# Infini-attention and feed-forward block: score maxima from 32-row products of the high parts, softmax sums from the numerators

## The chip, the cores and the metric

The kernel runs on one core of a Trainium2 chip. The metric is the device time of one execution in microseconds (us); lower is better. A core has five engines that matter here, each working through its own instructions in order: TensorE (PE in the profile, with its weight loads shown apart as PEld), VectorE (DVE), ScalarE (ACT), GpSimd (POOL), and SyncE (SP), which in this kernel issues the DMA transfers.

## The reference

A transformer block on 2048 tokens of width 1024. A modulation vector scales and shifts a layer norm; then attention with 32 heads of width 32, in four segments of 512 tokens, each with a compressed memory of the segments before; an output product; a second norm; a gated feed-forward of width 3584. What the change touches is the softmax of one segment:

```
for s in range(N):
    qs, ks, vs = q[:, :, s], k[:, :, s], v[:, :, s]
    logits = jnp.einsum("bhqd,bhkd->bhqk", qs, ks) * scale + mask
    p = _softmax(logits, axis=-1)
    a_dot = jnp.einsum("bhqk,bhkd->bhqd", p, vs)
    ...
    a_mem = num / den
    o = g * a_mem + (1.0 - g) * a_dot
```

## The kernel before, in words

All activations stand transposed, with the feature in the partitions. Products that need precision are made of high and low parts: a float32 number is cut into a rounded part (hi, type fp32r) and the rest (lo), and hi*hi, hi*lo and lo*hi are summed. An fp32r product streams its columns once; plain float32 products (the ones with `pt`, `mz`, `pk`) stand in the profile as two instructions for each product.

Attention is done in 32 steps: four heads (a group, 128 features) by one segment of 512 tokens. Round n of the loop in `attention` interleaves three things: the projections of step n+1 (`K0` to `K7` keys and values, `Q0` to `Q3` queries), the scores and maxima of step n (`scores`), and the probabilities and outputs of step n-1 (`values`), with the memory's products, the cuts of later weights, and in some rounds norms and loads of other stages. The order in a round is written out by hand, token by token, in `ORDER`; one string of tokens sets the order in each engine's queue at once, SP's and POOL's too.

The tokens that matter, with their lines:

- `kt` (`turned`, L412 to L421): the keys are transposed on PE; ACT writes the high part `kh`, DVE the low part `kl`. `qo` (`parts`, L442 to L451) does the same for the queries.
- `dk`, `dq` (`spread`, L403 to L406): three DMA transfers each put high, high and low parts into rows 0, 3, 6, ... and 1, 4, ... and 2, 5, ... of the first 96 partitions of `ks` and `qs`, so that one product over 96 rows sums the three partial products for one head. The weights' columns are arranged (`by_head`) so that the four heads of a group lie in the free dimension there.
- `S0` to `S3` (`rows`, L530 to L545): for 128 queries and each of four heads, one product over 96 rows with 256, 256, 384 or 512 keys (L540), then DVE adds the mask and takes the row's maximum (L542, output in `sj`, and the accumulator's result in `mm`), then ACT takes the exponential with that maximum and sums it into `ll` (L544). Each of the four writes a PSUM bank of its own, out of five that all small products share (`s_ps`).
- `tm`, `tq` (`maxima` L547, `to_queries` L557): the maxima, cut in two parts, are turned and put by DVE into rows 96 to 127 of `qs` (L559), which meet selecting rows in `ks`.
- `tr` (`shares` L563): one over the sums, times one minus the gate, spread on ACT (L568).
- `T0` to `T3` (L626 to L636): the scores again, transposed, keys in the partitions, over all 128 rows, so that the maximum is subtracted by the product itself; ACT takes the exponential into `pt` (L633), POOL clears the half above the diagonal (L634).
- `P0`, `P2` (`PV`, L638 to L644): values times `pt`, four heads side by side in four groups of 32 array columns (L643), 64 such groups of products in all.
- `rt` (`factors`, L652): PE turns the shares (L649) and ACT copies them; `rm` (L656) multiplies the output by them; `yt` adds the memory's part; `zs` stores.

`PV` is the only place in which products with fewer than 128 output rows lie side by side; `S` is the only one with fewer than 128 contraction rows (96).

## Time and profile before

| | us |
|---|---|
| median of 3 runs | 2741.93 (2741.18 to 2743.84) |
| profiled execution | 2742.03 |
| its span in the profile | 2740.3 |
| 28 of the 32 attention steps, 101.4 to 894.0 | 792.6 |
| PE busy in these | 792.03 |
| DVE busy in these | 555.40 |
| ACT busy in these | 579.28 |

The span is the time from the first to the last profiled instruction. Busy time is the union of an engine's instructions; since PE's instructions overlap in its pipeline, a busy PE may still wait inside, and what an instruction costs there is read from the distance between starts. The attention steps run from about 65 us to 980 us; what follows is the output product, the second norm and the feed-forward, which the change doesn't touch.

### The profile page before, as it was taken

The numbers are of one execution on the slowest core, as the hardware profiler recorded it, in microseconds if no ns is written. First come the engines' busy times: TensorE is split into PE (matmuls) and PEld (weight loads), VectorE is DVE, ScalarE is ACT, GpSimd is POOL, SyncE is SP. The second block draws the span as 40 slices with busy tenths as digits, with TensorE's granted clock in tenths as the row PEclk, the third lists the DMA queues.
The fourth block names the chain that finished last, engine by engine and source line by source line (L and its number), as shares of the span: only waits on it lengthen the run. The fifth ranks groups of instructions, "written<-read, shape, count | busy, mean of one in ns | idle before, by whom it ended". The sixth has DMA issues, their size and how long they took to land.

```text
span 2740.3 us, 43048 instructions
## 1 busy us (share of the span) xinstructions
PE 2715.1 (99%) x14748; PEld 2284.0 (83%) x14748; DVE 1556.0 (57%) x3516; ACT 1202.7 (44%) x2811; POOL 852.5 (31%) x1446
## 2 busy tenths in 40 slices
PE   7999999999999999999999999999999999999999
PEld 6888888888888888888888888888888888888887
DVE  7677667666776745555555555334433254575456
ACT  6777777676767634333333233111111033233323
POOL 4333334433333534254455452443541000000000
PEclk9999999999999999999999999999999999999999
DMA  7454445435443568778898678999998687795563
GB/s 261 131 148 135 129 126 150 125 108 151 113 131 101 158 210 295 251 290 326 310 351 310 263 281 276 361 362 353 363 358 313 219 316 252 264 307 197 185 207 123
DMA packets 244890, 637.77 MB, mean 233 GB/s; under 512 B 24768, under 2 KB 49344, under 8 KB 244672
## 3 DMA queue, kind: packets, MB, share of 16 engines
q1 hardware_dynamic: 244672, 635.03, 68.1%
q8 instruction: 116, 1.90, 0.3%
q14 instruction: 102, 0.84, 0.1%
HBM read 372.79 MB, written 211.81 MB: 213 GB/s over the span
## 4 chain that ended last, share of the span: by engine, by line
PE 96%; DMA 2%; DVE 1%; issue 0%; POOL 0%; ACT 0%; SPq 0%; DVEq 0%; POOLq 0%; ACTq 0%
PE f L1139 37%; PE y L1353 19%; PE kv L383 12%; PE y L714 6%; PE q L389 6%; PE S L540 3%; PE T L631 3%; PE O L643 3%; PE num L599 1%; PE M L582 1%; PE kv L512 1%; DMA ru<-wu 1%; PE tpb L266 1%; PE kT L417 0%; PE R L649 0%
## 5 line engine op out<-in xcount | busy, mean ns | idle before, releaser
L1139 PE MATMUL f<-A,B 128*128 128x512 f32 x4704 | 1072.7, 390 | 0.4 <-DVE c L1164 0.4
L1139 PEld LDWEIGHTS f<-A,B 128*128 128x128 f32 x4704 | 881.4, 188 | 184.8 <-DVE c L1164 1.1
L1353 PE MATMUL y<-B,L 128*128 128x512 f32 x2352 | 533.3, 389 | 0.0
L1353 PEld LDWEIGHTS y<-B,L 128*128 128x128 f32 x2352 | 441.4, 188 | 91.7
L544 ACT ACTIVATE sj<-sj,mm 128x384 f32<-128x384 f32 (+3 forms) x512 | 281.4, 552 | 49.4 <-DVE mm L542 49.1
L542 DVE CUSTOM_DVE_ANT_0 sj<-S,mask 128x384 f32<-128x384 f32 (+3 forms) x512 | 228.0, 488 | 106.2 <-PE S L540 81.3
L634 POOL TENSOR_SCALAR_AFFINE_SELECT pt<-pt 128x128 f32<-128x128 f32 x512 | 164.1, 345 | 293.9 <-ACT pt L633 287.6
L853 ACT ACTIVATE L<-X 128x512 fp32r<-128x512 f32 x168 | 105.8, 630 | 257.2 <-PE y L1353 167.0
L633 ACT ACTIVATE pt<-T 128x256 f32<-128x256 f32 (+3 forms) x512 | 181.9, 443 | 69.3 <-PE T L631 63.5
L383 PE MATMUL kv<-w,hhh 128*128 128x256 f32 x1024 | 199.6, 285 | 0.0
L855 DVE TENSOR_TENSOR L<-X,L 128x512 fp32r<-128x512 f32 x168 | 115.9, 691 | 145.8 <-ACT L L853 145.6
L1173 ACT ACTIVATE g<-g 128x512 f32<-128x512 f32 x56 | 35.4, 631 | 369.4 <-DVE g L1172 369.4
L374 POOL TENSOR_TENSOR w<-r,w 128x256 fp32r<-128x256 f32 x180 | 134.2, 781 | 158.6 <-ACT w L368 156.9
L383 PE MATMUL kv<-w,hha 128*128 128x256 f32 x896 | 177.4, 286 | 1.9 <-DVE vx L401 1.9
L1078 POOL TENSOR_TENSOR rw<-rw,gbb 128x256 f32<-128x256 f32 x112 | 91.4, 853 | 248.6 <-DMA rw<-wd 184.8
L383 PEld LDWEIGHTS kv<-w,hhh 128*128 128x128 f32 x1024 | 164.8, 191 | 1.4 <-issue 0.4
L383 PEld LDWEIGHTS kv<-w,hha 128*128 128x128 f32 x896 | 145.8, 192 | 4.1 <-DVE vx L401 2.2
L383 PE MATMUL kv<-w,hlh 128*128 128x256 f32 x512 | 144.7, 283 | 0.0
L383 PE MATMUL kv<-w,hla 128*128 128x256 f32 x448 | 127.0, 283 | 0.0
L714 PE MATMUL y<-wo,hho 128*128 128x512 f32 x384 | 125.9, 394 | 0.0
L1160 ACT ACTIVATE g<-f 128x512 f32<-128x512 f32 x56 | 33.5, 598 | 206.0 <-PE f L1139 206.0
L540 PE MATMUL S<-ks,qs 96*128 96x256 f32 (+2 forms) x512 | 110.4, 333 | 0.3
(244 smaller groups left out, 4150.1 us busy)
## 6 DMA issues: line engine op xcount, KB each, us to landing
bc_d<-B SPq DMA_DIRECT2D x189, 512.0 KB, 5.4
...
X<-hid_d SPq DMA_DIRECT2D x112, 256.0 KB, 4.8
wr<-gd_d SPq DMA_DIRECT2D x84, 256.0 KB, 4.1
qs<-qh SPq DMA_DIRECT2D x64, 256.0 KB, 3.6
```

Of the source, the lines that this page charges most:

```text
L374: nc.gpsimd.tensor_sub(w[:, 1, c], r[:, c], f32(w[:, 0, c]))
L383: nc.tensor.matmul(ps, b[:, sl], w[:, a], start=(kt == 0 and a == 0 and b is hi), stop=(kt == KT - 1 and a == 1), **kw)
L389: nc.tensor.matmul(ps, w[:, a], b, start=(kt == 0 and a == 0 and b is hi), stop=(kt == KT - 1 and a == 1), **kw)
L540: nc.tensor.matmul(ps[:, :nk], qs[:96, j, i * P:(i + 1) * P], ks[:96, j, :nk], start=True, stop=True)
L542: nc.vector.tensor_tensor_reduce(out=sj[:, :nv], in0=ps[:, :nv], in1=mask[:, L - nv:], scale=-1.0, scalar=3.4e38, op0=ALU.add, op1=ALU.min ...
L544: nc.scalar.activation(sj[:, :nv], sj[:, :nv], AF.Exp, bias=mm[:, j, i:i + 1], scale=-1.0, accum_out=ll[:, i, j:j + 1])
L633: nc.scalar.activation(pt, ps[:, nn - n:nn], AF.Exp)
L634: nc.gpsimd.affine_select(pt[:, :P], pt[:, :P], pattern=[[1, P]], compare_op=ALU.is_ge, fill=0.0, base=0, channel_multiplier=-1)
L714: nc.tensor.matmul(ps, b[:, i * P:(i + 1) * P], w[:, a, g % 2], start=(g == 0 and a == 0 and b is hi), stop=(g == G - 1 and a == 1))
L855: eng.tensor_sub(lo[:, k], src[:, k], f32(hi)[:, k])
L1139: nc.tensor.matmul(ps, B[m, i][:, a, kt * P:(kt + 1) * P], A[p, i, kt][b], start=(start and kt == 0 and a == 0 and b == 0), stop=(kt == 3 ...
L1353: nc.tensor.matmul(banks[t], ops[k][:, y, t * P:(t + 1) * P], B[slots[k]][:, x], start=(i not in (2, 4, 3) and j == 0 and x == 0 and y == ...
```

## The change

- `S` multiplies the high parts alone, straight from `kh` and `qh` (32 rows for each head, at partitions 0, 32, 64 and 96), with no copies by DMA. The columns of the weights are arranged so that a head's 32 features lie together. DVE adds the mask and takes the maximum as before, but writes its main output back to PSUM; `sj`, ACT's exponentials of it, and `ll` are gone. The maximum need not be exact, since numerators and sum now use the same one.
- The sums come from the numerators: `p1` to `p3` add `pt` of the later key blocks to that of the first (DVE), and `rt` multiplies them by a matrix of ones (four heads in four groups of 32 array columns). DVE turns the result, takes the reciprocal and turns it back; `rm` multiplies by it and by one minus the gate (`omc`). `tr`, the turns and the copies of the shares are gone.
- `dk`, `dq` now write the parts to DRAM (`aside`); the transfers into `ks` and `qs` (`fk`, `fq`) follow a round later and read from DRAM, 256 KB each.
- `tq` moves from DVE to ACT.
- `pt` has four tags of exact sizes; high and low parts have tags of their own.
- All orders are written anew.

The diff, with the old orders left out:

```diff
@@ -152,6 +152,7 @@
     omg = pa.tile([P, H], F32, name="omg")
+    omc = pa.tile([P, G], F32, name="omc")
     ones = cs([P, P], "ones")
@@ -348,7 +349,7 @@
-    hT, W, Mst, ST, SC, SY, PK = {}, {}, {}, {}, {}, {}, {}
+    hT, W, Mst, ST, HI, SY, PK, LATE = {}, {}, {}, {}, {}, {}, {}, {}
     ks_t = []
@@ -400,10 +401,14 @@
-    def spread(dst, parts):
-
-        for row, part in parts:
-            nc.sync.dma_start(f32(dst[row:96:3]), f32(part))
+    def aside(tiles, nm):
+        for c in "hl":
+            t = tiles[c + "d"] = dram.tile([P, L], F32, name=f"{c}{nm}_d", tag=nm[0] + c, bufs=2)
+            nc.sync.dma_start(t, f32(tiles[c]))
+
+    def spread(dst, tiles, rows):
+        for row, c in rows:
+            nc.sync.dma_start(f32(dst[row:96:3]), tiles[c + "d"].rearrange("(j d) t -> d j t", j=4))
@@ -415,8 +420,9 @@
                 nc.tensor.transpose(ps[:, t * P:(t + 1) * P], kn[:, t], ident)
-            kh = tiles["h"] = t2("kh" + nm, "sp", bufs=4, dt=F32R)
-            kl = tiles["l"] = t2("kl" + nm, "sp", bufs=4, dt=F32R)
+            kh = tiles["h"] = t2("kh" + nm, "hi", bufs=3, dt=F32R)
+            kl = tiles["l"] = t2("kl" + nm, "lo", bufs=2, dt=F32R)
+            HI.setdefault(n, {})["k"] = kh
             nc.scalar.activation(kh, ps, AF.Copy)
@@ -432,7 +438,8 @@
         u["kt"] = turned
-        u["dk"] = lambda: spread(ks, ((0, tiles["h"]), (1, tiles["h"]), (2, tiles["l"])))
+        u["dk"] = lambda: aside(tiles, "k" + nm)
+        LATE[n, "k"] = lambda: spread(ks, tiles, ((0, "h"), (1, "h"), (2, "l")))
         u["ek"] = expo
@@ -441,14 +448,14 @@
             ps = get()
-            qh = tiles["h"] = t2("qh" + nm, "sp", bufs=4, dt=F32R)
-            ql = tiles["l"] = t2("ql" + nm, "sp" if n else "sj", bufs=4 if n else 3, dt=F32R)
+            qh = tiles["h"] = t2("qh" + nm, "hi", bufs=3, dt=F32R)
+            ql = tiles["l"] = t2("ql" + nm, "lo", bufs=2, dt=F32R)
+            HI.setdefault(n, {})["q"] = qh
             nc.scalar.activation(qh, ps, AF.Copy, scale=SCALE)
...
             nc.vector.scalar_tensor_tensor(ql, ps, SCALE, f32(qh), op0=ALU.mult, op1=ALU.subtract)
-            ST[n][0] = t2("qs" + nm, "qs", bufs=2, dt=F32R, shape=(P, 4, L))
@@ -460,7 +467,12 @@
         u["qo"] = parts
-        u["dq"] = lambda: spread(ST[n][0], ((0, tiles["h"]), (2, tiles["h"]), (1, tiles["l"])))
+        u["dq"] = lambda: aside(tiles, "q" + nm)
+        def late():
+            ST[n][0] = t2("qs" + nm, "qs", bufs=2, dt=F32R, shape=(P, 4, L))
+            spread(ST[n][0], tiles, ((0, "h"), (2, "h"), (1, "l")))
+
+        LATE[n, "q"] = late
         u["ea"] = expo
@@ -528,21 +540,19 @@
         def rows(i):
-            qs, ks = ST[n][:2]
+            qh, kh = HI[n]["q"], HI[n]["k"]
             if i == 0:
                 d["mm"] = t2("mm" + nm, "mm", bufs=2, shape=(P, 4, 4))
-                d["ll"] = t2("ll" + nm, "ll", bufs=2, shape=(P, 4, 4))
-            mm, ll = d["mm"], d["ll"]
+            mm = d["mm"]
             nk = max(256, (i + 1) * P)
             nv = (i + 1) * P
+            ps = [s_ps(f"S{nm}_{j}{i}") for j in range(4)]
             for j in range(4):
-                ps = s_ps(f"S{nm}_{j}{i}")
-                nc.tensor.matmul(ps[:, :nk], qs[:96, j, i * P:(i + 1) * P], ks[:96, j, :nk], start=True, stop=True)
-                sj = t2(f"sj{nm}_{j}{i}", "sj", bufs=3)
-                nc.vector.tensor_tensor_reduce(out=sj[:, :nv], in0=ps[:, :nv], in1=mask[:, L - nv:], scale=-1.0,
+                h = slice(DH * j, DH * (j + 1))
+                nc.tensor.matmul(ps[j][:, :nk], qh[h, i * P:(i + 1) * P], kh[h, :nk], start=True, stop=True)
+            for j in range(4):
+                nc.vector.tensor_tensor_reduce(out=ps[j][:, :nv], in0=ps[j][:, :nv], in1=mask[:, L - nv:], scale=-1.0,
                                                scalar=3.4e38, op0=ALU.add, op1=ALU.min, accum_out=mm[:, j, i:i + 1])
-                nc.scalar.activation(sj[:, :nv], sj[:, :nv], AF.Exp, bias=mm[:, j, i:i + 1], scale=-1.0,
-                                     accum_out=ll[:, i, j:j + 1])
@@ -556,23 +566,14 @@
             for i in range(4):
-                nc.vector.tensor_scalar(ST[n][0][96:128, :, i * P:(i + 1) * P],
-                                        d["tt"][96:128].unsqueeze(1).to_broadcast([32, 4, P]),
-                                        seli[96:128, i:i + 1], None, op0=ALU.mult)
-
-        def shares():
-            rc = t2("rc" + nm, "rc", bufs=2, shape=(P, 4, 4))
-            nc.vector.reciprocal(rc, d["ll"])
-            nc.vector.tensor_mul(rc, rc, omg[:, 4 * g:4 * g + 4].unsqueeze(1).to_broadcast([P, 4, 4]))
-            rx = t2("rx" + nm, "rx", shape=(P, 4, 4, DH))
-            nc.scalar.activation(rx, rc.unsqueeze(3).to_broadcast([P, 4, 4, DH]), AF.Copy)
-            SC[n] = [rx, None]
+                nc.scalar.activation(ST[n][0][96:128, :, i * P:(i + 1) * P],
+                                     d["tt"][96:128].unsqueeze(1).to_broadcast([32, 4, P]),
+                                     AF.Identity, scale=seli[96:128, i:i + 1])
...
         u["tq"] = to_queries
-        u["tr"] = shares
@@ -629,7 +630,7 @@
                 nc.tensor.matmul(ps[:, :nn], ks[:, j, kc * P:(kc + 1) * P], qs[:, j, L - nn:], start=True, stop=True)
-                pt = t2(f"pt{nm}_{j}{kc}", f"pt{kc % 2}", bufs=4, shape=(P, L - kc % 2 * P))[:, :n]
+                pt = t2(f"pt{nm}_{j}{kc}", f"pt{kc}", bufs=4, shape=(P, n))
                 nc.scalar.activation(pt, ps[:, nn - n:nn], AF.Exp)
@@ -649,12 +650,24 @@
+        def added(kc):
+            for j in range(4):
+                t = pts[0, j][:, kc * P:]
+                nc.vector.tensor_add(t, t, pts[kc, j])
+
         def factors():
+            ps = s_ps("l" + nm)
+            for j in range(4):
+                nc.tensor.matmul(ps[32 * j:32 * j + 32], ones[:, :DH], pts[0, j], start=True, stop=True,
+                                 skip_group_check=True)
             d["r"] = tmp_tile("R" + nm)
-            nc.scalar.activation(d["r"], turned(SC[n][0], "R"), AF.Copy)
+            nc.vector.transpose(d["r"], ps)
+            rc = t2("rc" + nm, "rc", bufs=2, shape=(P, 16))
+            nc.vector.reciprocal(rc, d["r"].rearrange("p (b r) -> p b r", r=32)[:, :, 0])
+            nc.vector.transpose(d["r"], rc.unsqueeze(2).to_broadcast([P, 16, 32]))
...
         def scaled():
-            nc.vector.tensor_mul(d["r"], d["o"], d["r"])
+            nc.vector.scalar_tensor_tensor(d["r"], d["o"], omc[:, g:g + 1], d["r"], op0=ALU.mult, op1=ALU.mult)
@@ -663,6 +676,8 @@
         u["P2"] = lambda: PV(2)
+        for kc in (1, 2, 3):
+            u[f"p{kc}"] = lambda kc=kc: added(kc)
         u["rt"] = factors
@@ -1414,54 +1429,54 @@
...
+            "fk fq N K K N G1 K N N G2 K G0 K S0 S1 C1 S2 K S3 C2 K l1 l2 A tm tq L1 K K L2 K",
         (1,):
...
+            "fk K0 T0 ns K1 T1 K2 K3 K4 S0 P0 D0 o0 nc T2 p1 mz K5 p2 T3 K6 p3 n0 n1 m0 A rt Q0 nd S1 P2 K7 S2 m1 Q1 Q2 "
+            "rm S3 o1 fq yt zs Q3 kt qo tm nu ek ea ne dn dk nl tq dq eb",
         (2, 4, 6, 8):
...
+            "K0 K1 K2 Q0 S0 K3 G2 S1 fk ns wd o0 Q1 G1 T0 Q2 T1 Q3 nc C2 S2 P0 T2 K4 p1 T3 p2 qo fq G0 K5 C1 S3 ea p3 l2 "
+            "tm K6 P2 n0 eb n1 nd L2 nl l1 A K7 rt o1 rm kt dk ne L1 ek tq yt zs wl dq",
         (3, 5, 7):
...
+            "K0 K1 K2 S0 K3 T0 ns D0 K4 S1 K5 m0 T1 o0 A P0 p1 m1 mz T2 K6 T3 Q0 fk p2 nc S2 K7 p3 Q1 S3 P2 rt o1 Q2 nu "
+            "Q3 wl wd fq qo n0 tm ea n1 rm nl kt dn nd ek dk ne tq eb yt zs dq",
         (9,):
...
+            "K0 K1 K2 D0 S0 mz K3 T0 o0 K4 S1 K5 m0 T1 Q0 m1 S2 fk fq P0 T2 p1 Q1 S3 K6 Q2 p2 Q3 tm T3 K7 P2 p3 o1 kt rt "
+            "qo ea dk eb rm nu A dn ek dq yt zs tq",
         (10, 12):
...
+            "K0 G2 G1 K1 K2 S0 K3 A T0 C1 K4 wd S1 K5 o0 T1 Q0 S2 P0 T2 Q1 T3 K6 fk C2 p1 p2 p3 fq l2 S3 K7 P2 o1 kt dk "
+            "L2 l1 G0 rt L1 Q2 Q3 wl rm tm qo ea ek yt eb wl tq dq zs",
         (11, 13):
...
+            "D0 K0 S0 m0 wd K1 K2 T0 K3 S1 mz Q0 o0 fk Q1 S2 m1 wd K4 T1 Q2 S3 P0 wl p1 Q3 T2 K5 T3 p2 qo p3 fq tm ea K6 "
+            "eb K7 rt P2 o1 dq kt rm A ek tq yt dk nu zs dn",
         (14,):
...
+            "x wd wd K0 x K1 G2 x T0 K2 T1 x P0 x fk p1 T2 C2 x K3 G1 o0 l2 p2 S0 x K4 K5 T3 p3 S1 x P2 K6 x K7 S2 rt x "
+            "Q0 Q1 x o1 C1 x L2 kt fq dk S3 l1 x Q2 x G0 Q3 rm tm A qo ek dq L1 yt zs ea tq eb",
         (15,):
...
+            "K0 K1 S0 x D0 K2 fk A K3 S1 K4 S2 K5 fq m0 x x o0 T0 Q0 x T1 x Q1 mz m1 S3 P0 tm p1 Q2 T2 Q3 T3 p2 wd p3 K6 "
+            "qo x ea P2 K7 nu o1 dn dq eb kt rt tq rm yt dk x zs ek",
         (16,):
...
+            "x G1 x K0 Q0 T0 mz wl Q1 x T1 x Q2 S0 P0 x fk T2 p1 C1 G2 K1 S1 Q3 p2 K2 fq T3 l1 K3 wd p3 P2 qo o0 ea L1 S2 "
+            "K4 K5 S3 wl K6 G0 rt eb C2 tm K7 A rm nu o1 kt tq dk yt wl dq zs l2 L2 ek dn",
         (17,):
...
+            "fk K0 K1 K2 D0 m0 S0 T0 wd K3 S1 Q0 T1 Q1 m1 mz o0 S2 P0 p1 T2 p2 K4 T3 K5 p3 S3 K6 fq rt Q2 tm Q3 qo ea K7 "
+            "eb P2 o1 rm kt yt ek dq dk nu dn zs tq",
         (18, 20, 22, 24, 26, 28):
...
+            "K0 K1 K2 S0 K3 S1 wd K4 G1 T0 C1 G2 mz K5 S2 o0 K6 T1 P0 T2 Q0 fk T3 p1 K7 C2 p2 p3 S3 P2 o1 rt rm kt l1 fq "
+            "yt Q1 ek dk l2 Q2 tm nu dn Q3 G0 qo ea tq L2 zs wl L1 eb A dq",
         (19, 21, 23, 25, 27):
...
+            "wl D0 K0 K1 S0 K2 wd mz T0 wd K3 T1 K4 S1 P0 T2 p1 p2 K5 m0 T3 p3 K6 S2 P2 fk K7 wl o0 rt S3 o1 m1 Q0 Q1 rm "
+            "kt Q2 tm yt Q3 qo ea ek fq nu dn dk zs dq eb tq",
         (29,):
...
+            "K0 K1 S0 D0 wd K2 m0 m1 T0 K3 T1 K4 mz S1 P0 T2 K5 T3 p1 p2 K6 p3 o0 S2 Q0 P2 S3 Q1 rt K7 Q2 o1 tm rm fk kt "
+            "Q3 yt nu fq qo ea dk dn zs ek tq eb dq",
         (30,):
...
+            "x x K0 wo fk K1 S0 K2 ga mz wd T0 x x wo x K3 x o0 T1 fq K4 S1 P0 T2 p1 ga T3 p2 Q0 p3 x ga S2 P2 Q1 wp rt "
+            "wl K5 wp S3 x K6 K7 Q2 o1 wo Q3 x tm rm qo kt yt ea ek nu wl x dn x dk zs eb A dq tq x x wl wo",
         (31,):
...
+            "K0 K T0 T1 wp K1 S0 fk Q0 P0 wp T2 p1 S1 mz K2 p2 T3 S2 p3 K3 fq P2 K4 K5 S3 rt K6 rm yt tm Q1 nu tq dn zs "
+            "Q2 K7 K Q3",
         (32,):
...
+            "K0 K1 T0 K2 Q0 Q1 T1 K3 P0 T2 p1 p2 K4 T3 K5 p3 Q2 P2 rt rm yt K6 zs K7 Q3",
     }
@@ -1479,7 +1494,7 @@
             for h in range(2):
-                tag, bufs = ("pt0", 4) if h == 0 else ("sj", 3) if i < 3 else ("pq", 2)
+                tag, bufs = ("pt0", 4) if h == 0 else ("hi", 3) if i < 3 else ("pq", 2)
                 t = t2(f"x0_{i}_{h}", tag, bufs=bufs)
@@ -1515,6 +1530,9 @@
         nc.vector.tensor_scalar(omg, gall, -1.0, 1.0, op0=ALU.mult, op1=ALU.add)
+        own = omg.rearrange("p (g j) -> p g j", j=4)
+        nc.vector.tensor_mul(own, own, sel4.unsqueeze(1).to_broadcast([P, G, 4]))
+        nc.vector.tensor_reduce(omc, own, axis=AX.X, op=ALU.add)
         row = row_parts(scb, scol, tmp_tile, "sc")
@@ -1607,6 +1625,8 @@
             if n < len(steps):
+                for c in "kq":
+                    u["f" + c] = LATE.pop((n, c), None) or (lambda n=n, c=c: LATE.pop((n, c))())
                 scores(u, n, *steps[n][1:])
@@ -1648,7 +1668,7 @@
         pick = tmp_tile("pick")[:, :P].rearrange("p (j d) -> p j d", d=DH)
-        nc.gpsimd.affine_select(pick, ones.rearrange("p (j d) -> p j d", d=DH), pattern=[[-1, 4], [-4, DH]],
+        nc.gpsimd.affine_select(pick, ones.rearrange("p (j d) -> p j d", d=DH), pattern=[[-DH, 4], [-1, DH]],
                                 compare_op=ALU.is_equal, fill=0.0, base=0, channel_multiplier=1)
@@ -1692,7 +1712,7 @@
     def by_head(w):
-        return np.asarray(w).reshape(D, G, 4, DH).transpose(0, 1, 3, 2)
+        return np.asarray(w).reshape(D, G, 4, DH)
```

32 lines of the change are left out of this document (removed).

## The prediction

> **What bounds the kernel now.** I read the page first: its busy shares and the chain that ended last.
>
> ```profile
> span 2740.3 us, 43048 instructions
> PE 2715.1 (99%) x14748; PEld 2284.0 (83%) x14748; DVE 1556.0 (57%) x3516; ACT 1202.7 (44%) x2811; POOL 852.5 (31%) x1446
> PE 96%; DMA 2%; DVE 1%; issue 0%; POOL 0%; ACT 0%; SPq 0%; DVEq 0%; POOLq 0%; ACTq 0%
> ```
>
> PE is busy nearly all the span and holds 96% of the chain. Then the stretches: the 28 attention steps from 101.4 to 894.0 us, by busy time (PE, PEld, DVE, ACT, POOL), clock, DMA share.
>
> ```profile
> 101.40:894.00 792.60, 792.03 (x5898) 692.90 (x5897) 555.40 (x1841) 579.28 (x1658) 287.62 (x667) 1.00 0.46 130
> ```
>
> A step takes 792.6 / 28 = 28.3 us; DVE works 19.8 of it, ACT 20.7. "Busy" PE overlaps in its pipeline, so I asked the timeline what products cost from start to start.
>
> ```profile
> 601.39 0.28 PE L383 MATMUL kv<-w,hhh 128*128 128x256 f32 x1
> 601.51 0.64 PE L540 MATMUL S<-ks,qs 96*128 96x256 f32 x4
> 602.00 0.40 PE L389 MATMUL q<-hhh,w 128*128 128x512 f32 x1
> 602.23 0.40 PE L389 MATMUL q<-hlh,w 128*128 128x512 f32 x1
> ...
> 613.64 0.28 PE L383 MATMUL kv<-w,hlh 128*128 128x256 f32 x1
> 613.76 0.28 PE L383 MATMUL kv<-w,hhh 128*128 128x256 f32 x1
> 613.97 0.86 PE L643 MATMUL O<-pt,vx 128*32 128x256 f32 x16
> 614.76 0.49 PE L599 MATMUL num<-mz,pq 128*128 128x132 f32 x2
> ```
>
> A 256-column product takes 0.12 us, one of 512 columns 0.23; I take 0.175 for 384. Four `S` of 256 columns follow a `kv` product and are followed by `q` without a gap: 602.00 - 601.51 = 0.49. So `S` costs 4 x (0.12 + 0.12 + 0.175 + 0.23) = 2.58 us a step. `T` has the same shapes.
>
> `O` (values times numerators) is different. It has 32 output columns for each head, four heads side by side.
>
> ```profile
> 604.62 0.16 PEld L643 LDWEIGHTS O<-pt,vx 128*32 128x32 f32 x8 [0.25 <-issue]
> 604.62 1.71 PE L643 MATMUL O<-pt,vx 128*32 128x512 f32 x16
> 605.07 0.13 PEld L643 LDWEIGHTS O<-pt,vx 128*32 128x32 f32 x4 [0.30 <-issue]
> 605.50 0.13 PEld L643 LDWEIGHTS O<-pt,vx 128*32 128x32 f32 x4 [0.30 <-issue]
> ```
>
> By source line, durations in ns as least/median/most:
>
> ```profile
> L643 PE MATMUL O<-pt,vx x1024: 272/445/617, 88.1 to 975.2; 128*32 128x512 f32 x43, 128*32 128x256 f32 x43, 128*32 128x128 f32 x43, 128*32 128x384 f32 x42
> L599 PE MATMUL num<-mz,pq x192: 273/276/380, 90.0 to 953.8; 128*128 128x132 f32 x192
> ```
>
> The weights of four heads are loaded together (eight loads in 0.16 us), and the loads stand ahead of each pass, so a float32 product of 512 columns for four heads takes two passes, 605.07 - 604.62 = 0.45 and 605.50 - 605.07 = 0.43. But entering and leaving this arrangement costs. Entering: the last `kv` is fed in until 613.76 + 0.12 = 613.88, `O` starts at 613.97, 0.09 later. Leaving: `O`'s last pass (128 columns, the shortest form, 0.27 us) starts at 613.97 + 0.86 - 0.27 = 614.56, is fed in until 614.67, and `num` starts at 614.76: 0.09 again. The first product after it also shows its own weight load: 0.38 where the median of `num` is 0.276, 0.104 more. With 0.02 for the first small load, a visit costs 0.09 + 0.02 + 0.09 + 0.104 = 0.31 us, 64 visits 20 us. A step then adds up to about 28.0 us of products and visits; some 0.3 us are waits. PE is bound by its own instructions, so the change is worth what it does to those.
>
> **The change part by part.** `S` becomes 16 products of 32 rows, four in four row groups. No row of this trace has such a product; `O` is nearest, the only one that lies side by side. If row groups behave like its column groups, a group of four costs 0.09 (enter) + 0.104 (first load, 128 columns now) + 0.02 (stagger) + one product's columns + 0.09 + 0.104 (leave) = 0.41 + columns. Four groups: 1.63 + 0.645 = 2.28 a step, against 2.58: 32 x 0.30 = -9.7 us. From below the cost is the columns alone (no visit cost, 0.02 stagger each): 0.73, -59 us. From above, loads one behind another: 3 x 0.104 more in each of 128 groups, +40 on the first value. I take `O`'s value.
>
> The Trainium skill, TensorEngine Tiling (Array Packing), Key Properties, says that changing the tiling mode, not just the tile, drains TensorE; it lists 32-row modes beside 32-column ones. That speaks against the change, and the gaps of 0.09 around `O` agree for columns; no run here shows rows.
>
> Where two such groups are neighbours in the queue, one leaving and loading (0.2 us) falls away. In the new strings I count 48 places where an `S` token stands next to another `S`, `P0`, `P2` or `rt` among tokens with PE work (three for each odd round from 19 to 27, one each even round from 18 to 28): -9.6 us.
>
> `rt` loses four turns, and gains the product with ones: plain float32, 512 columns, 32 output columns a head, so `O`'s first two passes, 0.88 us a step, 28.2 us. Twenty times `rt` stands beside neither `P0` nor `P2`: 20 x 0.31 = 6.2 us. The turns, on the timeline and by source line:
>
> ```profile
> 603.39 0.60 PE L649 MATMUL R<-ident,rx 128*128 128x128 f32 x4
> L649 PE MATMUL R<-ident,rx x128: 270/272/329, 87.5 to 965.8; 128*128 128x128 f32 x128
> ```
>
> Start to start (0.60 - 0.272) / 3 = 0.109, four of them 0.44 a step, -14.0 us. PE's sum is -9.7 - 9.6 + 28.2 + 6.2 - 14.0 = +1.1 us: what the row groups save is spent on the product with ones.
>
> The other engines decide what is waited for.
>
> ```profile
> L544 ACT ACTIVATE sj<-sj,mm 128x384 f32<-128x384 f32 (+3 forms) x512 | 281.4, 552 | 49.4 <-DVE mm L542 49.1
> L544 ACT ACTIVATION_READ_ACCUMULATOR sj<-sj,mm 128x1 f32 x512 | 96.4, 188 | 0.0
> L568 ACT ACTIVATE rx<-rc 128x512 f32<-128x512 f32 x32 | 20.2, 631 | 46.9 <-DVE rc L566 46.9
> L654 ACT ACTIVATE R<-R 128x512 f32<-128x512 f32 x32 | 19.8, 620 | 8.4 <-PE R L649 8.3
> L1531 ACT ACTIVATE x<-x,mr,rsa 128x512 f32<-128x512 f32 x8 | 6.1, 803 | 2.4 <-DVE mr L1528 2.4
> ```
>
> ACT loses (281.4 + 96.4) / 32 = 11.8 us a step and 0.63 and 0.62, and gains the four of `tq`, between the 0.52 that DVE takes for one (below) and the 0.80 of a scaled 512-column copy (L1531): 2.1 to 3.2 us. It falls from 20.7 to about 10 us.
>
> ```profile
> L1258 DVE TENSOR_TENSOR X<-X,X 128x512 f32<-128x512 f32 x28 | 19.1, 684 | 0.0
> L566 DVE TENSOR_TENSOR rc<-rc,omg 128x16 f32<-128x16 f32 x32 | 6.3, 198 | 1.1
> L565 DVE RECIPROCAL rc<-ll 128x16 f32<-128x16 f32 x32 | 7.8, 244 | 0.1
> L555 DVE STREAM_TRANSPOSE tt<-mt 32x32 f32<-32x32 f32 x128 | 26.3, 205 | 2.4
> L559 DVE TENSOR_SCALAR qs<-tt,seli 32x512 fp32r<-32x512 f32 x128 | 59.1, 520 | 1.0
> L421 DVE TENSOR_TENSOR kl<-kT,kh 128x512 fp32r<-128x512 f32 x32 | 22.0, 688 | 6.9 <-ACT kh L420 6.6
> ```
>
> DVE gains twelve additions a step. On the line through L566 (16 columns, 198 ns) and L1258 (512, 684) they take 0.558, 0.433 and 0.307 us; four of each, 5.2 us. It gains two turns of 128x512: no row has one; the ends are 0.2 (L555, as if columns were free) and 16 x 0.205 = 3.3, and I take 0.68, what L1258 takes for as many columns: 1.37. With a reciprocal of 0.24, less `tq` (59.1 / 32 = 1.85) and `tr` (0.44): +4.5, from 19.8 to 24.3 of 28.3 us. Writing the masked scores to PSUM instead of `sj` stands in no row; reading PSUM costs 4 ns (L421 against L1258), so I take nothing, with 0.25 us each as the far end, at which DVE's 4 us of room are gone, and the loss of the wait for `sj` (below) as the other.
>
> Waits, by waiter and what it waited for (us in total, times, longest):
>
> ```profile
> PEld S L540 <- DVE mm L542: 5.4, 13, 0.6
> DVE sj L542 <- ACT sj L544: 19.5, 32, 1.0
> ```
>
> I take it that the first goes with the second: `S` waits for PSUM banks that DVE empties late because ACT still reads `sj`. So -5 us. New waits: `p1` writes the tile that `P0` reads, so DVE waits for PE there, and the next `S`'s maxima queue behind it; `rt`'s product waits on PE for `p3`, with everything behind it. In round 18 there are `S3` and `P2` between them, about 1.2 us of PE's work against 1.2 us of `p3`; cover gone, it costs as much as DVE is late. All waits together: from -9 us (none left) to +16 (half a us a step).
>
> The transfers cost nothing:
>
> ```profile
> ks<-kh SPq DMA_DIRECT2D x64, 256.0 KB, 3.7
> oT_d<-R SPq DMA_DIRECT2D x32, 256.0 KB, 4.3
> ```
>
> `dk` writes in one round, `fk` reads in the next, and `T` needs it in the third, against 3.7 and 4.3 us to land. `S` no longer waits for any of them, but no wait of PE for them showed. Four more issues of 256 KB a step stand in SP's queue, ahead of the stores and loads of the same round, and 0.46 of the DMA engines' time is taken. If the cover went, `T0` would wait 8 us once, in the first rounds.
>
> **The sum.** The profiled execution took 2742.03 us, 1.7 more than its span, and 0.1 more than the median of the three runs, 2741.93. 2742.0 + 1.1 - 5 = 2738 us. With the bounds on waits and some of the visits, this case alone runs from 2728 to 2757. A measurement of this kernel can tell 0.2%, 5.5 us: below 2736.4 is faster, above 2747.4 slower.
>
> **The rivals.** *Row groups cost no visit.* For it: 96 rows (601.51 to 602.00) cost none, and the gaps around `O` may belong to its columns alone. Then `S` is -59 us, nothing is saved by neighbours: -59 + 34.4 - 14.0 - 5 = -44, 2698 us. By the Trainium skill, TensorE: Matmul & The Clock Gate, Part 3, four products of 32 rows and 512 columns were measured 3.07 times as fast packed; as an estimate, 82.6 / 3.07 = 26.9 us for `S`, and 2702. No run here shows it.
>
> *Weights load one behind another.* Slower. `O`'s loads have 32 columns and each goes to other columns; `S`'s four have 128, over the same columns in other rows. If each waits for the one before, 128 groups cost 0.31 more, +40: 2778. It decides from 0.07 us a group on, a quarter of that price: 128 x 0.07 = 9 us takes 2738 over the bound of 2747.4. Against it: `O`'s eight loads start within 0.06 us.
>
> *Nothing runs side by side.* Each product waits for its own bank, out of five, and the first free one starts alone; `S` keeps 2.58 and pays 1.63 of visits: +52 instead of -9.7, 2800. The change would not do what it says. Against it: ACT and DVE empty banks sooner.
>
> *DVE becomes the bound.* If a turn costs 3.3 us, DVE has 24.3 + 5.2 = 29.5 us a step, 1.2 more than PE had: +39, 2780. Against it: 128 columns of `mt` turn as four of 205 ns, most of which is start-up.
>
> **How the numbers follow.** The forecast has 0.53: 0.21 below 2736.4, 0.20 within, 0.12 above. No visit cost 0.25, all faster; loads in turn 0.11, nothing side by side 0.04, DVE the bound 0.07, all slower. Faster 0.46, same 0.20, slower 0.34. The range goes from 2692, a little below the free row groups, to 2782, above loads in turn and a full DVE; left out are 2800, and the ends of the outer cases, under 0.2.
>
> **What would show it.** `S`'s four products start within 0.03 us of one another, with a gap of about 0.09 on both sides, no load ahead, and the next product about 0.1 longer; a gap without it speaks for the first rival, starts 0.1 apart for the second. The product with ones takes two passes of 0.43 to 0.45. DVE shows about 24 us a step, ACT about 10. The forecast is wrong if attention's 28 steps change by more than 13 us, and by which term is to be read from `S`'s distance between starts.

## The result and the profile after

The changed kernel takes 2780.05 us (median of 4 runs, 2778.66 to 2784.03), the kernel before 2741.55 beside it: ratio 1.0141, 95% interval 1.0124 to 1.0159. It is 38.5 us slower. The forecast was 2738 us, no change; the time lies inside the range of 2692 to 2782, on the side of the slower rivals. The page of the changed kernel (its profiled execution took 2778.66 us):

```profile
span 2777.0 us, 42793 instructions
PE 2737.9 (99%) x14876; PEld 2235.9 (81%) x14876; DVE 1717.3 (62%) x3806; ACT 970.7 (35%) x1851; POOL 881.4 (32%) x1446
PE 93%; DVE 3%; DMA 2%; issue 1%; POOL 0%; ACT 0%; SPq 0%; DVEq 0%; ACTq 0%; POOLq 0%
```

PE stays "99% busy", but DVE has grown by 161 us and now holds 3% of the chain instead of 1%. Where do the 37 us of span lie? I cut both spans at the first `T` of step 0, the first `T` of the last step, and the first feed-forward product. Windows of before, then of after: length, busy time of PE, PEld, DVE, ACT, POOL, clock, DMA share, GB/s.

```profile
0.00:82.30 82.30, 62.09 (x384) 53.70 (x385) 61.15 (x163) 57.16 (x103) 34.05 (x57) 0.97 0.63 225
82.30:962.50 880.20, 879.47 (x6461) 765.24 (x6461) 616.42 (x2028) 640.08 (x1824) 329.17 (x752) 1.00 0.46 133
962.50:1126.50 164.00, 164.00 (x782) 134.25 (x781) 82.68 (x153) 57.33 (x106) 57.47 (x82) 1.00 0.79 255
```

```profile
0.00:84.60 84.60, 64.17 (x384) 54.62 (x385) 57.75 (x158) 50.65 (x74) 33.15 (x57) 0.91 0.63 228
84.60:992.30 907.70, 896.67 (x6574) 713.58 (x6573) 770.47 (x2308) 415.67 (x894) 358.44 (x751) 0.99 0.57 165
992.30:1163.50 171.20, 167.63 (x797) 136.38 (x796) 90.37 (x171) 58.00 (x108) 59.31 (x83) 1.00 0.76 245
1163.50:2777.00 1613.50, 1609.47 (x7125) 1331.27 (x7124) 798.75 (x1173) 446.34 (x776) 430.52 (x556) 1.00 0.80 285
```

The opening grew by 2.3 us, attention by 27.5, the stretch after it by 7.2; the feed-forward is unchanged (2740.3 - 1126.5 = 1613.8 before).

First the forecast's sign for `S`. The timeline of the changed kernel around one group of 256 columns, and around the product with ones (`l`):

```profile
266.06 0.28 PE L384 MATMUL kv<-w,hha 128*128 128x256 f32 x1
266.27 0.39 PE L552 MATMUL S<-kh,qh 32*128 32x256 f32 x4
266.59 0.39 PE L384 MATMUL kv<-w,hha 128*128 128x256 f32 x1
266.82 0.28 PE L384 MATMUL kv<-w,hla 128*128 128x256 f32 x1
...
281.74 1.04 PE L661 MATMUL l<-pt,ones 128*32 128x512 f32 x8
282.71 0.50 PE L390 MATMUL q<-hha,w 128*128 128x512 f32 x1
```

The four products stand in one row because they start together: in the trace 3 ns apart. The last `kv` is fed until 266.06 + 0.12 = 266.18 and `S` starts 0.09 later; the next product starts 0.32 after `S` and takes 0.23 instead of 0.12. So a group of 256 columns costs 0.09 + 0.32 + 0.11 = 0.52 us, more than the four products in a row of before (0.49), and the gain is in the wider ones: over the trace the 0.32 is 0.37 for 384 columns and 0.44 for 512. A step's four groups cost 2 x 0.52 + 0.57 + 0.63 = 2.24 us, forecast 2.28, against 2.58. That is 1.15 times as fast where the columns alone would be almost four times. This speaks for the rule weighed in the prediction (the Trainium skill, TensorEngine Tiling (Array Packing), Key Properties: a change of mode drains TensorE): the gap of 0.09 us stands on both sides of row groups as of column groups. The 3.07 of the Trainium skill, TensorE: Matmul & The Clock Gate, Part 3, is not what such groups bring here, where each stands alone between full products: 1.15. The product with ones, `l`, costs 282.71 - 281.74 = 0.97, less the 0.09 of leaving 0.88, as forecast.

Next the other engines. The 28 rounds from the first `T` of step 1 to that of step 29, before and then after:

```profile
112.90:900.20 787.30, 786.73 (x5864) 687.60 (x5863) 551.57 (x1824) 575.06 (x1643) 287.62 (x667) 1.00 0.46 131
```

```profile
123.00:929.30 806.30, 797.04 (x5938) 637.69 (x5937) 684.15 (x2064) 370.49 (x799) 312.79 (x667) 1.00 0.57 162
```

DVE works 684.15 / 28 = 24.4 us a step (forecast 24.3), of now 28.8. But single terms differ. By line and shape, busy us and mean ns:

```profile
L656 DVE TENSOR_TENSOR pt<-pt,pt 128x384 f32<-128x384 f32 x124 | 72.1, 641 | 6.1 <-PE O L644 6.1
L656 DVE TENSOR_TENSOR pt<-pt,pt 128x256 f32<-128x256 f32 x124 | 58.3, 528 | 4.4 <-POOL pt L635 4.4
L656 DVE TENSOR_TENSOR pt<-pt,pt 128x128 f32<-128x128 f32 x124 | 52.7, 483 | 3.3 <-POOL pt L635 3.3
L667 DVE STREAM_TRANSPOSE R<-rc 128x512 f32<-128x512 f32 x31 | 22.1, 711 | 1.1
L554 DVE CUSTOM_DVE_ANT_0 S<-S,mask 128x512 f32<-128x512 f32 x128 | 84.2, 717 | 11.7 <-PE S L552 11.7
L554 DVE DVE_READ_ACCUMULATOR2_ANT mm<- 128x1 f32 x511 | 71.4, 140 | 0.0
```

An addition takes 641, 528 and 483 ns where I had 558, 433 and 307: 6.6 us a step for twelve, not 5.2. The turn takes 0.71 (I took 0.68, and 3.3 was the rival's price). Writing to PSUM, which I took at nothing, puts 0.03 us on each reduction (start to start 648 ns for 512 columns, 612 before), 0.5 us a step.

And what PE waits for, in the attention steps (55 to 1030 us):

```profile
PEld O L644 <- POOL pt L635: 18.2, 58, 0.7
PEld S L552 <- DVE mm L554: 8.3, 16, 0.8
PEld T L632 <- ACT pt L634: 5.7, 10, 0.9
PE T L632 <- ACT pt L634: 3.4, 8, 0.6
```

`T` waits for ACT, though ACT has less work than before. The timeline shows why that name misleads:

```profile
469.66 3.51 DVE L656 TENSOR_TENSOR pt<-pt,pt 128x256 f32<-128x256 f32 x4
...
471.50 0.28 PE L632 MATMUL T<-qs,ks 128*128 128x256 f32 x1
...
471.88 0.28 ACT L634 ACTIVATE pt<-T 128x128 f32<-128x128 f32 x1 [2.36 <-PE T L632]
...
472.20 0.38 PE L632 MATMUL T<-qs,ks 128*128 128x256 f32 x1 [0.43 <-ACT pt L634]
...
473.01 0.38 PE L632 MATMUL T<-qs,ks 128*128 128x256 f32 x1 [0.43 <-ACT pt L634]
473.10 0.29 DVE L554 CUSTOM_DVE_ANT_0 S<-S,mask 128x128 f32<-128x128 f32 x1
```

ACT had been idle for 2.36 us. DVE does four additions until 473.1 (3.5 us), and only then comes to the four banks that `S` filled. Four of the five are full, so `T` has one, and its products go one by one with ACT's copy between them, 0.8 us apart instead of 0.12.

To put it all in one sum I took, for each product of those 28 rounds, the distance to the next product's start, and added these up by kind:

| us in 28 rounds | before | after | without additions (below) |
|---|---|---|---|
| `S` | 78.6 | 47.0 | 42.6 |
| `l` | 0 | 30.0 | 27.4 |
| `R` (turned shares) | 12.5 | 0 | 0 |
| `O` | 72.3 | 79.8 | 73.1 |
| `T` | 75.4 | 86.2 | 82.9 |
| all else | 548.5 | 563.3 | 561.1 |
| sum | 787.3 | 806.3 | 787.1 |

"All else" holds the first product behind each group, whose own weight load now shows. It also lacks 34 products, 5 to 6 us, that fall outside the cut since the first `T` stands elsewhere in the new rounds. `O` and `l` grow where a head's numerators come late and the four products no longer start together: `l` starts head by head in four of the 28 rounds, and takes 1.65 us there instead of 1.00.

What PE must do stayed about the same. With `S` at 42.6 and `l` at 27.4, their values without the additions, it is -36.0 + 27.4 - 12.5 + 14.8 = -6.3 us in the cut, and about -1 with the 34 products. What the others make PE lose is then up to 4.4 (`S`) + 2.6 (`l`) + 7.5 (`O`) + 10.8 (`T`) = 25.3 us; in `T` some loads behind a group are counted with it.

### The profile page after: what moved, and what is told of

It reads as the page before. It is cut to its first block, busy times and chain, and to the rows that moved or that the text cites. A ratio compares the mean times of both kernels' runs of the same rounds, so it can differ in the third digit from the quotient of the medians.

```text
span 2777.0 us, 42793 instructions
## 1 busy us (share of the span) xinstructions
PE 2737.9 (99%) x14876; PEld 2235.9 (81%) x14876; DVE 1717.3 (62%) x3806; ACT 970.7 (35%) x1851; POOL 881.4 (32%) x1446
## 4 chain that ended last, share of the span: by engine, by line
PE 93%; DVE 3%; DMA 2%; issue 1%; POOL 0%; ACT 0%; SPq 0%; DVEq 0%; ACTq 0%; POOLq 0%
PE f L1154 38%; PE y L1368 19%; PE kv L384 12%; PE q L390 6%; PE y L729 5%; PE T L632 3%; PE O L644 3%; PE S L552 2%; PE l L661 1%; PE kv L524 1%; PE M L583 1%; PE num L600 1%; DVE S L554 1%; PE kT L422 1%; PE tpb L267 0%
## 5 line engine op out<-in xcount | busy, mean ns | idle before, releaser
L635 POOL TENSOR_SCALAR_AFFINE_SELECT pt<-pt 128x128 f32<-128x128 f32 x512 | 189.6, 393 | 381.6 <-ACT pt L634 374.9
L554 DVE CUSTOM_DVE_ANT_0 S<-S,mask 128x384 f32<-128x384 f32 (+3 forms) x512 | 235.5, 521 | 76.1 <-PE S L552 76.0
L384 PE MATMUL kv<-w,hhh 128*128 128x256 f32 x1024 | 205.8, 288 | 0.9 <-DVE vx L402 0.9
L656 DVE TENSOR_TENSOR pt<-pt,pt 128x256 f32<-128x256 f32 (+2 forms) x384 | 185.6, 547 | 14.4 <-POOL pt L635 7.8
L632 PE MATMUL T<-qs,ks 128*128 128x256 f32 (+2 forms) x512 | 114.2, 340 | 5.6 <-ACT pt L634 3.4
L632 PEld LDWEIGHTS T<-qs,ks 128*128 128x128 f32 x512 | 82.5, 192 | 35.0 <-issue 16.1
```

What stands on the lines that cost most here:

```text
L384: nc.tensor.matmul(ps, b[:, sl], w[:, a], start=(kt == 0 and a == 0 and b is hi), stop=(kt == KT - 1 and a == 1), **kw)
L554: nc.vector.tensor_tensor_reduce(out=ps[j][:, :nv], in0=ps[j][:, :nv], in1=mask[:, L - nv:], scale=-1.0, scalar=3.4e38, op0=ALU.add, op1=A ...
L632: nc.tensor.matmul(ps[:, :nn], ks[:, j, kc * P:(kc + 1) * P], qs[:, j, L - nn:], start=True, stop=True)
L635: nc.gpsimd.affine_select(pt[:, :P], pt[:, :P], pattern=[[1, P]], compare_op=ALU.is_ge, fill=0.0, base=0, channel_multiplier=-1)
L656: nc.vector.tensor_add(t, t, pts[kc, j])
```

## The experiments

Theory A: VectorE, 24.4 of 28.8 us busy and in order, comes late to the full banks and the numerators, and TensorE waits. Rival B: taking four of five banks at once costs this whatever VectorE's load. Rival C: the new orders are at fault. All times are beside the kernel before on the same chip.

**Without the additions** (the sums hold only the first key block).

```diff
             for j in range(4):
-                t = pts[0, j][:, kc * P:]
-                nc.vector.tensor_add(t, t, pts[kc, j])
+                pass
```

> The changed kernel without the twelve additions of a step (p1 to p3 do nothing; the sums then hold the first key block alone). Theory A, VectorE works 24.4 us of a 28.8 us step and is late, so that PSUM banks with unreduced scores make TensorE wait (about 26 us in attention): 6.6 us of VectorE's work a step go, the waits fall under 8 us, and the time to 2752 to 2760 us. Rival B, the waits come from S taking four of five banks at once, whatever VectorE's load: they stay, 2772 to 2780 us. Rival C, the waits lie in the order of the tokens (an engine stands at a token whose input comes late): 2772 to 2780 us too.

2760.66 us, ratio 1.0061 (1.0045 to 1.0078): 19 us of the 38 are back, 0.7 us above the range that A asked for.

```profile
123.80:910.70 786.90, 781.55 (x5938) 631.90 (x5937) 535.61 (x1728) 369.46 (x799) 272.46 (x667) 1.00 0.58 166
```

DVE falls to 19.1 us a step and the 28 rounds to 786.9, nearly the time of before. The table's last column says how: 4.4 us of `S`, 3.3 of `T`, 6.7 of `O`, 2.6 of `l`, 2.2 of all else. So the cause is the additions, but the products that wait for banks (`S` and `T`, 7.7 us) are less than half of its way to PE; `O` and `l`, which start head by head, are 9.3. Not all of the loss goes: between the cuts used above, attention takes 886.0 us here, 21.7 less than in the changed kernel and still 5.8 more than before, and the stretch behind it is 10.0 longer than before.

**Additions on GpSimd**: `nc.gpsimd.tensor_add` in place of `nc.vector.tensor_add`.

> The twelve additions on GpSimd instead of VectorE. Theory A: VectorE falls to about 18 us a step, GpSimd rises from 11 to about 20 (0.78 us for 256 columns, so 4 x (1.1 + 0.78 + 0.43) = 9 us more), the waits mostly go: 2755 to 2768 us. If GpSimd's lateness takes the place of VectorE's (the next pt wait behind additions): 2780 or more. Rivals B and C: 2775 to 2785 us.

2961.59 us, ratio 1.0800 (1.0784 to 1.0816). What PE's loads wait for, between 100 and 960 us:

```profile
PEld l L661 <- POOL pt L656: 58.7, 62, 5.7
PEld O L644 <- POOL pt L635: 41.3, 52, 5.8
```

At the median an addition of 384, 256 and 128 columns takes GpSimd 1.01, 0.73 and 0.46 us. Now GpSimd is late, with `l` and `O` behind it. Part of the loss are slower products: the mean granted clock is 0.975, against 0.996 in the changed kernel. The run moves the fault to another engine and tells nothing between A and B.

**The reduction's output to SBUF**, into one tile of two-byte elements (the 130-column memory tiles go from 11 buffers to 9 to make room).

```diff
+            sj = t2(f"sj{nm}_{i}", "sj", dt=mybir.dt.bfloat16)
...
-                nc.vector.tensor_tensor_reduce(out=ps[j][:, :nv], in0=ps[j][:, :nv], in1=mask[:, L - nv:], scale=-1.0,
+                nc.vector.tensor_tensor_reduce(out=sj[:, :nv], in0=ps[j][:, :nv], in1=mask[:, L - nv:], scale=-1.0,
```

> The masked scores go to a bfloat16 scratch tile in SBUF instead of back to PSUM (only the row maxima are used). In the trace the 512-column reduction takes 717 ns with PSUM output against 686 before, and its accumulator read 140 against 83. Theory A: VectorE gets 16 x 0.04 to 0.09 = 0.6 to 1.4 us a step back, and waits fall by 3 to 12 us: 2768 to 2777 us. Rivals B and C: 2778 to 2782 us.

2806.85 us, ratio 1.0233 (1.0217 to 1.0248): slower, a miss. Each instruction did get shorter (688 for 717 ns, the accumulator's read 83 for 140), but all write one tile, and each now waits until the one before has ended. Two reductions of 128 columns:

```profile
265.97 0.29 DVE L555 CUSTOM_DVE_ANT_0 sj<-S,mask 128x128 bf16<-128x128 f32 x1
266.18 0.08 DVE L555 DVE_READ_ACCUMULATOR2_ANT mm<- 128x1 f32 x1
266.40 0.29 DVE L555 CUSTOM_DVE_ANT_0 sj<-S,mask 128x128 bf16<-128x128 f32 x1
```

From start to start that is 0.44 us, where the changed kernel's trace has 0.25; the other sizes show the same 0.19 to 0.2. Sixteen a step are 3.1 us more of VectorE's time, and the kernel is 27 us slower than the changed one. I had meant to shorten the suspect and lengthened it. That VectorE's time counts is shown by it, as A says; but longer reductions also hold the banks longer, so it doesn't tell A from B.

**Row groups alone**: the kernel before with `S` in row groups, the parts copied through DRAM and the columns arranged as in the change, but sums from ACT as before, and the old orders; `sj` has two buffers.

> The kernel before with the row groups alone: S from the high parts in four row groups, four banks at once, in the old orders; the sums still from ScalarE's exponentials of S (so they are slightly inexact), parts copied through DRAM. By the distances in the changed kernel's trace S with its visits costs 2.23 us a step against 2.58: -11 us. Theory A: VectorE's load is the old one (19.8 us a step), so no new waits: 2726 to 2738 us. Rival B, four banks at once make TensorE wait: 2745 us or more.

2763.89 us, ratio 1.0080 (1.0065 to 1.0095). DVE's waits between 100 and 960 us, before and here:

```profile
DVE sj L542 <- ACT sj L544: 18.5, 31, 1.0
```

```profile
DVE sj L549 <- ACT sj L551: 50.1, 149, 1.1
```

With two `sj` instead of three DVE waits for ACT, and holds the banks. That is my third buffer missing, not the row groups, so nothing follows for B. **With three `sj`** (mask in two-byte elements and 9 memory tiles, for room):

> The kernel before with the row groups alone, as in the last such run, but with three score tiles as before instead of two (a bfloat16 mask makes the room); the sums still from ScalarE's exponentials. In the last run VectorE waited 50 us for ScalarE's two tiles, against 18.5 us before, and TensorE's waits came to 18 us. Theory A, VectorE's lateness alone makes the waits: with the third tile it empties the banks as before, and only TensorE's saving is left: 2728 to 2742 us. Rival B, four banks taken at once: waits stay, 2752 us or more.

2738.21 us, ratio 0.9988 (0.9978 to 0.9998). `DVE sj <- ACT sj` is down to 10.8 us. The 28 rounds:

```profile
112.20:892.20 780.00, 778.61 (x5863) 648.46 (x5862) 551.10 (x1824) 574.53 (x1643) 286.87 (x667) 1.00 0.53 170
```

DVE works 19.7 us a step, as before, and four banks are taken at once all the same. The rounds are 7.3 us shorter: the distances of `S` went from 78.6 to 48.4, and all else rose by 22.9. My term of -9.7 for 32 steps makes -8.5 for 28. So B falls as the main cause, but not to nothing: between 100 and 960 us PE's loads of `S` wait 9.0 us for DVE in 21 places, before 4.1 in 8. Of the 7.3 only 3 to 4 reach the end; the stretch behind attention takes 167.6 us here instead of 164.0.

**The new sums alone**: before, with `p1` to `p3` and the new `rt` put into the old orders by rule (each addition behind the `T` that it needs, `rt` after `p3`), `S` unchanged in 96 rows, and one `sj`.

> The kernel before with the new sums alone: S over 96 rows as before, its exponentials on ScalarE left out, twelve additions and the product with ones in the old orders (p1 to p3 put behind T2 and T3, rt behind P2). TensorE's sum: +28 for the product with ones, -14 for the turns, no visit more, +14 us. VectorE: the additions at the measured 641, 528 and 483 ns are 6.6 us, the two turns and the reciprocal 1.7, tr gone 0.4, tq still on VectorE: 19.8 + 7.9 = 27.7 of 28.3 us. Theory A: large waits, 2785 to 2830 us. Rival B (row groups and banks make the waits): 2752 to 2762 us.

2908.65 us, ratio 1.0604 (1.0588 to 1.0620), well over what either expected. It has the fault of one `sj` as well, so its size can't be read as the price of the sums. **The whole change in the old orders**, with the new tokens placed by the same rule (PSUM output as in the change):

> The changed kernel in the old orders (fk and fq at the head of a round, p1 behind T2, p2 and p3 behind T3, rt behind P2, tr gone). Theory A: VectorE's load is the same, and the old orders leave no room for the additions: 2780 to 2820 us. Rival C, the new orders themselves are at fault: 2750 to 2765 us.

2868.40 us, ratio 1.0457 (1.0441 to 1.0472). DVE's work is that of the change (667.76 us in the 28 rounds), and the time 88 us longer. In those rounds `O` takes 98.3 us, `T` 93.6, `S` 62.5 and `l` 38.7, and the granted clock is 0.97 where it was 1.00. So the new orders are not what slows the change, they avoid most of what it would cost. C falls in attention, and A has to be put more narrowly: it isn't the sum of DVE's work that counts, but when in the round the additions keep it from the banks and the numerators. C is right outside attention: from the first `T` of the last step to the feed-forward this run takes 165.0 us, the changed kernel 171.2.

**VectorE relieved elsewhere**: in the changed kernel the value copies go to ACT, and each feature map uses ACT's Relu, so that DVE does one instruction instead of two.

```diff
-        nc.vector.tensor_copy(vx[:, t:t + n, :P], psv[:, :, P:])
+        nc.scalar.activation(vx[:, t:t + n, :P], psv[:, :, P:], AF.Copy)
...
-                nc.vector.tensor_scalar_min(e, e, 1.0)
...
+                nc.scalar.activation(pkf, knf, AF.Relu)
+                nc.vector.scalar_tensor_tensor(pkf, e, 1.0, pkf, op0=ALU.min, op1=ALU.add)
```

> The changed kernel with some of VectorE's work on ScalarE, which is busy 13 of 28.8 us: the copies of the values (2 x 0.41 a step), and the maximum with zero, so that one VectorE instruction instead of two makes each of the two feature maps (0.42 and 0.5 in three steps of four). VectorE falls by 1.5 us a step, 24.4 to 22.9. Theory A: a share of what the additions cost, 1.5 / 6.6 of 19 us, 4 us or a little more: 2768 to 2777 us. Rival C: 2778 to 2784 us, more if ScalarE's tokens stand at late inputs.

2773.42 us, ratio 1.0104 (1.0087 to 1.0120): 6.6 us back for 1.2 us a step less of DVE, as A expects.

**Without GpSimd's clearing** of the half above the diagonal (numerators hold later keys):

```diff
-                nc.gpsimd.affine_select(pt[:, :P], pt[:, :P], pattern=[[1, P]], compare_op=ALU.is_ge, fill=0.0,
-                                        base=0, channel_multiplier=-1)
```

> The changed kernel without GpSimd's clearing of the half above the diagonal (numerators then hold later keys too). In its trace an addition that runs while GpSimd is idle takes 280, 418 and 548 ns (128, 256, 384 columns), one under a GpSimd instruction 373, 505 and 640 in the middle and up to 1092. Theory A with sharing between the two engines as the reason why additions were dearer than forecast: VectorE gets up to 1.6 us a step back, and 6 to 10 us of the time, 2768 to 2776 us; the additions' means fall towards 300, 430 and 560 ns. If the additions keep their durations, GpSimd is not the reason, and the time stays within 5 us of 2780.

2761.51 us, ratio 1.0072 (1.0055 to 1.0089). The additions get cheaper, most of all the narrow ones:

```profile
L654 DVE TENSOR_TENSOR pt<-pt,pt 128x384 f32<-128x384 f32 x116 | 65.3, 624 | 5.8 <-PE O L642 5.8
L654 DVE TENSOR_TENSOR pt<-pt,pt 128x256 f32<-128x256 f32 x116 | 45.3, 451 | 0.0
L654 DVE TENSOR_TENSOR pt<-pt,pt 128x128 f32<-128x128 f32 x116 | 26.5, 289 | 1.0
```

289 and 451 ns are close to my 307 and 433; the widest stay at 624, because 23 of the 128 still run beside an instruction of GpSimd, mostly one with two inputs such as the cuts of weights, and take 1.09 us at the median, against 0.55 for the others. In the changed kernel's trace the additions of 128, 256 and 384 columns take 281, 418 and 548 ns while GpSimd is idle, so the price was right for VectorE alone. At the median of all that run beside one of GpSimd's instructions they take 373, 505 and 640; the clearing adds some 0.09 us to one, GpSimd's two-input instructions add some 0.53. The clearing itself takes 393 ns on average in the changed kernel, 313 in the one without additions. The Trainium skill has a rule for it that the prediction left out: SBUF — State Buffer, "SBUF: two separate sides", says that GpSimd, where it reads that memory, and a VectorE instruction with two SBUF inputs hold one pair of ports in turn, each for a whole instruction. These numbers show that each lengthens the other; they do not show the taking of turns.

The gain of 18.5 us is more than this, though: in the 28 rounds `O` falls from 79.8 to 69.7 and `l` from 30.0 to 27.4, because numerators now reach PE straight from ACT, while `T` falls from 86.2 to 84.4 alone. 2.6 us of `O`'s part lie below the kernel before and have nothing to do with the change.

**All relief at once** (the last two and no additions).

> The changed kernel with VectorE relieved as far as this study can: no additions (the sums then hold only the first key block), no affine_select (the numerators hold later keys), value copies and Relu on ACT. VectorE should work some 18 us of a step. If VectorE's lateness is all that the change lost, no T waits for ACT and the time is 2742 to 2750. If TensorE's own work or its order has grown as well, the waits are gone and the time still stays at 2752 to 2760.

2755.35 us, ratio 1.0050 (1.0037 to 1.0064), in the second case's range. The same cuts as above:

```profile
0.00:84.70 84.70, 63.61 (x385) 54.00 (x386) 56.07 (x152) 51.32 (x79) 33.09 (x57) 0.94 0.64 228
84.70:968.30 883.60, 877.70 (x6573) 706.25 (x6573) 566.61 (x1828) 455.94 (x1002) 178.16 (x255) 1.00 0.59 169
968.30:1139.90 171.60, 168.88 (x797) 137.04 (x796) 85.86 (x158) 57.84 (x107) 53.06 (x67) 0.99 0.76 242
```

Attention is within 3.4 us of before (with the 2.6 of `O` that no clearing gives), the opening and the stretch behind keep their 2.4 and 7.6. So these 10 us don't go with VectorE's work. In the stretch behind, 2.8 us are 12 products `y` that the old orders held inside attention, about 1 is the `l` of the last step, and one wait is 3.1 in the changed kernel and 2.7 in this run:

```profile
1144.37 0.70 SPq L714 DMA_DIRECT2D xr<-x  x1
1146.34 0.69 DVE L733 TENSOR_TENSOR xr<-y,xr 128x512 f32<-128x512 f32 x1 [2.40 <-DMA xr<-x]
...
1147.08 0.50 PE L729 MATMUL y<-wo,hho 128*128 128x512 f32 x1 [3.13 <-DVE xr L733]
```

The load of `xr` was issued late, and `y` waited for it. The opening is another matter. In the run with the additions on GpSimd it has the same code up to its end, the first `T`, and takes 79.5 us, less than before, at a granted clock of 0.99. In the changed kernel the granted clock between 67 and 74 us is 0.53, and 1.00 before; six blocks of projections between two `S` take 4.14 us there (67.41 to 71.55) and 2.13 before. So slower products alone make up the opening's 2.3 us, and that the new orders cost them is not shown; what lowers the clock there stays open. Waits also stay in the rounds of this run: `T` takes 80.9 us, before 75.4, and between 55 and 1030 us PE's loads of `S` and `kT` wait 5.3 and 5.0 us for DVE. Which token makes them was not tested.

**Two blocks in one visit**: row groups alone (three `sj`), with both 256-column blocks written side by side into the same four banks, so that a step has three visits for `S` instead of four.

```diff
+            if i == 1:
+                return
+            part = (0, 1) if i == 0 else (i,)
...
+            for k in part:
+                for j in range(4):
...
+                    c = slice(k * 256, k * 256 + 256) if i == 0 else slice(0, nk)
+                    nc.tensor.matmul(pss[j][:, c], qh[h, k * P:(k + 1) * P], kh[h, :nk], start=True, stop=True,
```

> Row groups alone in the old orders with three score tiles (2738.2 us in the last run), and the first two score blocks in one visit: S0 writes the 256 columns of both blocks into the two halves of the same four banks, and the token S1 is empty. TensorE saves one visit a step, 0.09 + 0.104 + 0.02 + 0.09 + 0.104 = 0.41 us, 13 us in all. Theory A, VectorE has room and no new wait comes: 2722 to 2730 us. If the longer stretch of eight reductions holds the banks too long (rival B): 2738 us or more.

2729.98 us, ratio 0.9959 (0.9944 to 0.9973): 11 us faster than the kernel before, and the fastest in this study.

```profile
264.67 0.28 PE L383 MATMUL kv<-w,hha 128*128 128x256 f32 x1
264.88 0.51 PE L549 MATMUL S<-kh,qh 32*128 32x256 f32 x8
265.32 0.39 PE L383 MATMUL kv<-w,hha 128*128 128x256 f32 x1
265.54 0.28 PE L383 MATMUL kv<-w,hla 128*128 128x256 f32 x1
```

Eight products take 0.09 + 0.44 + 0.10 = 0.63 us, where two visits took 1.04. **`S` behind `O`** as well: `S0` moved right behind `P0` in 21 rounds (18 by my count ahead of the run), with a projection between it and `T2`, to share a visit's edge.

```diff
-            ... Q2 P0 ns nc T2 Q3 T3 qo G2 n0 rt P2 K0 ea eb S0 C1 ...
+            ... Q2 P0 S0 ns nc Q3 T2 T3 qo G2 n0 rt P2 K0 ea eb C1 ...
```

> The same, and in the 18 rounds where S0 came some tokens behind P0 it now comes right behind it, so that leaving one arrangement and entering the other merge: 0.2 us each, 4 us. If nothing new waits, 2718 to 2727 us; if T2 then waits for banks, no gain or a loss of some us against the other run.

2802.40 us, ratio 1.0222 (1.0207 to 1.0238), a miss. PE's loads, 100 to 960 us:

```profile
PEld T L645 <- ACT pt L647: 23.8, 15, 3.8
PEld T L645 <- PE T L645: 22.8, 62, 0.7
```

Four banks now stay full through eight reductions, and `T2` and `T3` follow with one bank between them: the changed kernel's fault again, at DVE's old load. Where `S` stands before `T` counts for more here than a saved edge of 0.2 us.

## Why the prediction went wrong

Right: `S` costs 2.24 us a step (2.28), its products start together, and the visit has both its gaps of 0.09 and the 0.10 of the next load. So three rivals fell for the reason given: row groups do cost visits, weights do not load one behind another, and all four run side by side. `l` at 0.88 and the lost turns were right as well. With neighbours and lone visits, PE's own work was forecast at +1.1 us; measured about -1 in 28 of 32 rounds. The transfers cost nothing in attention. DVE's 24.3 us a step came out at 24.4.

Wrong: the step "So -5 us", with its bounds of -9 to +16 for all waits. I let the first wait (`S` for banks) go with its cause, and took the room of 4 us a step on DVE as enough. Measured, PE lost some 25 us in the 28 rounds (4.4 in `S`, 10.8 in `T`, 7.5 in `O`, 2.6 in `l`), as waits and as groups started head by head; the far bound was 16. Half a us a step was the most I gave to lateness, and it is 0.9. Two things in that step failed. It asked whether DVE's sum of work fits in a step, where each burst of additions (3.5 us in the timeline above) stands ahead of reductions that hold four of five banks. And the new waits that I named (`P0` before `p1`, `l` after `p3`) had no price of their own; `T`'s wait for a bank was not named at all.

Mis-sized beside it: the additions, at the median 0.37 to 0.64 us each where GpSimd works beside them and 0.28 to 0.55 alone, which made 6.6 us a step of 5.2. (In DVE's busy time, which counts overlapping instructions once, they are 5.9, so its sum hardly shows it.) And ACT came to 13.2 us a step, not about 10: the prediction took off the summed rows of L544, 11.8 us, which overlap and fill only 9.1. ACT had room left, so this cost nothing that shows.

The rival "DVE becomes the bound" named the engine and came within a us of the time, 2780. Its mechanism was not this: the turn costs 0.7, not 3.3, and DVE is idle 4.4 us a step. It is not a bound but late, and that the two times agree is luck.

Not foreseen: 9.5 us outside the attention steps. In the stretch behind, the products moved out of attention, the last `l` and one late load make up 6.9 of its 7.2; the first of these only changed place. The 2.3 of the opening are a lower granted clock, whose cause stays open.

Shown: the additions cost 19 us (1.0141 against 1.0061), through banks, `O` and `l` as split in the table; row groups alone cost nothing (0.9988, 0.9978 to 0.9998), and gain with two blocks in a visit (0.9959); the new orders are far better for these tokens than the old. Only argued: how the rest in attention, 5.8 us without any additions, divides between the banks held by `S` and the places of single tokens. That rival B has a small part in it is not ruled out.
